# Hash attention and a gated feed-forward on one core: block loads of q and k as two transfers of 64 partitions, with three small edits

## The chip, the core and the metric

The kernel runs on one core of a Trainium2 chip. The metric is the device time of one execution in microseconds (us); lower is better.

## What is computed

Attention with a hash mask, then a feed-forward network on its result. Per batch (4) and head (8), with 768 tokens of 64 numbers:

```python
q_bits = (np.einsum('bhsd,dk->bhsk', q, proj) > 0)      # 6 bits a token
k_bits = (np.einsum('bhsd,dk->bhsk', k, proj) > 0)
mask = q_bucket[:, :, :, None] == k_bucket[:, :, None, :]
scores = np.where(mask, scale * np.matmul(q, k.transpose(0, 1, 3, 2)), -1e9)
attn = softmax(scores);  x = np.matmul(attn, v)          # then (3072, 512)
xn = x / sqrt(mean(x * x) + 1e-6) * rms_g
g = xn @ w_gate;  val = xn @ w_val                       # 512 -> 1536
out = (g * sigmoid(g) * val) @ w_out                     # 1536 -> 512
```

Inputs and output are 32-bit floats; the matmuls run in 16-bit floats.

## The kernel before

**Units and slots.** The 3072 tokens are eight units `w` of 384 rows: unit w is one half of batch w // 2. A unit has 8 heads, handled as four pairs `hp`. Three slots make one head of one unit, each with two score matmuls and one exponential over 768 keys' third: 192 slots in all. What else happens is hung on slots by hand: `at(s, f, ..., rank)` puts a step into slot s, and a final loop runs the slots in order, so the order of every engine's instructions is written out by this list. Each engine runs its instructions in that order.

**How q and k come in.** A pair (b, hp) of batch and head pair has three raw tiles, k, q and v. For batch 0 and the first two pairs of batch 1 they are loaded in rows (`load_rows`, line 117) and turned by TensorE. For the other ten pairs, from (1, 2) to (3, 3), q and k come by `load_blocks` (line 127): the 128 partitions of the tile are four blocks of 32, one for each of the two heads and each half of the 64 numbers d; a partition holds 24 tokens of 32 numbers, so a transfer is made of pieces of 128 bytes. VectorE then turns 32 x 32 blocks (`turn_dve`, line 205, four steps each for k and q), GpSimd casts the result into the score operands `QK` (line 213), and TensorE, VectorE and SP make the hash bits: products (line 221), signs (line 228) and sends of 12 rows into `QK` (lines 259, 279, 297 and 319). The slots of loads, turns, casts and hashes of these pairs stand in the table `work`.

**SP's queue.** SP issues all loads of q, k and v, the sends of bits, the transposes of x and the stores, in the order of the slots. Raw tiles come from a pool of nine buffers. GpSimd issues the weight loads.

**The feed-forward of a unit.** From slot s0 = 24 w + 42 on: gate (`g_ps`, line 479) and value (`v_ps`, line 489) products for twelve parts of 128 columns, then the output products (`y_ps`, line 502) for three chunks `c` of 128 rows each, and a store of each chunk (line 513). Before that, `scale_x` normalizes x (lines 447 and 452) and `turn_x` turns it, a chunk at a time: by a DMA transpose on SP's queue for the units of the list `BY_DMA` (line 458), or by four TensorE transposes (line 464) and one VectorE multiply (line 465) for the others. Before, unit 0 alone goes by TensorE.

Of the kernel before, what the change touches and what calls it, by code (L numbers as in the profile page):

```python
# [41 lines left out]
BY_PE = [(0, hp) for hp in range(4)] + [(1, 0), (1, 1)]  # L42


BY_DMA = (1, 2, 3, 4, 5, 6, 7)


@with_exitstack
def kernel(
# [48 lines left out]
    def bank(name, shape=None, dt=FP32):  # L98
        return gps.tile(shape or [128, 512], dt, name=name, tag="g")
# [4 lines left out]
    def raw_tile(b, hp, which):  # L104
        shape = [128, 24, 32] if which != "v" and (b, hp) not in BY_PE else [128, 2, 6, D]
        raw[b, hp, which] = lpool.tile(shape, FP32, name=which + "L", tag="L")
        return raw[b, hp, which]
# [13 lines left out]
    def load_blocks(eng, b, hp, which):  # L121
        lt = raw_tile(b, hp, which)
        for hh in range(2):
            src = {"q": q, "k": k}[which][b, 2 * hp + hh].rearrange("(t k) d -> t k d", k=24)
            for dc in range(2):
                p0 = 64 * hh + 32 * dc
                eng.dma_start(out=lt[p0 : p0 + 32], in_=src[:, :, 32 * dc : 32 * dc + 32])

# [38 lines left out]
    def out_chunk(w, c):  # L169
        b, half = divmod(w, 2)  # L170
        return 2 * c + half if b < 2 else 3 * half + c
# [271 lines left out]
    def scale_x(w, c):  # L443
        if w not in xn:
            xn[w] = npool.tile([128, 3, DMODEL], FP16, name="xn")
        if w in BY_DMA:
            nc.vector.scalar_tensor_tensor(  # L447
                out=xn[w][:, c, :], in0=x[w][:, c, :], scalar=rstds[w][:, c : c + 1],
                in1=grow, op0=ALU.mult, op1=ALU.mult,
            )  # L450
        else:
            nc.vector.tensor_scalar_mul(xn[w][:, c, :], x[w][:, c, :], rstds[w][:, c : c + 1])

    def turn_x(w, c):
        if w not in xnT:
            xnT[w] = npool.tile([128, 4, HALF], FP16, name="xnT", bufs=2)
        if w in BY_DMA:
            nc.sync.dma_start(  # L458
                out=xnT[w][:, :, c * 128 : (c + 1) * 128], in_=xn[w][:, c, :], transpose=True,
            )  # L460
            return
        ps = bank("x_ps", [128, 4, 128], FP16)
        for kt in range(4):
            nc.tensor.transpose(ps[:, kt, :], xn[w][:, c, kt * 128 : (kt + 1) * 128], ident16)
        nc.vector.tensor_mul(
            xnT[w][:, :, c * 128 : (c + 1) * 128], ps,
            gcol.unsqueeze(2).to_broadcast([128, 4, 128]),
        )
# [24 lines left out]
        )  # L493

    obank = {}

    def project(w, c, f0, f1):
        if f0 == 0:
            obank[w, c] = bank("y_ps")
        y = obank[w, c]  # L500
        for ft in range(f0, f1):
            nc.tensor.matmul(  # L502
                y, ht[w][:, ft, c * 128 : (c + 1) * 128], wo[:, ft, :],
                start=(ft == 0), stop=(ft == NF - 1),
            )
        if f1 == NF:
            b, half = divmod(w, 2)
            ysb = spool.tile([128, DMODEL], FP32, name="ysb", bufs=3)
            nc.scalar.copy(ysb, y)  # L509
            rows = out[b * S : (b + 1) * S, :].rearrange("(p c) n -> p c n", c=6)  # L510

            def store():
                nc.sync.dma_start(out=rows[:, out_chunk(w, c), :], in_=ysb)

            if (w, c) == (1, 0):
                at(86, store, rank=8)
            else:
                store()
            del obank[w, c]
# [100 lines left out]
    def at(s, f, *a, rank=3):  # L620
        plan[s].append((rank, len(plan[s]), lambda: f(*a)))
# [63 lines left out]
    def in_row(loads, s, hash_slot=None):  # L685
        return loads, range(s, s + 8), (s + 4, s + 8, s + 9), hash_slot

    work = {
        (1, 2): in_row((31, 32, 45), 49, 58), (1, 3): in_row((41, 43, 50), 56, 65),
        (2, 0): in_row((53, 55, 60), 64), (2, 1): in_row((66, 67, 68), 73, 82),  # L690
        (2, 2): in_row((72, 75, 78), 82), (2, 3): in_row((79, 86, 87), 90, 99),
        (3, 0): in_row((88, 91, 98), 100), (3, 1): in_row((94, 97, 112), 110, 119),
        (3, 2): in_row((115, 118, 124), 126), (3, 3): in_row((122, 125, 137), 136, 145),
# [1 line left out]
    for (b, hp), (loads, turns, cast_slots, sh) in work.items():  # L695
        for which, s in zip("kqv", loads):
            at(s, load_rows if which == "v" else load_blocks, nc.sync, b, hp, which)
        for i, s in enumerate(turns):
            at(s, turn_dve, b, hp, "kq"[i // 4], i % 4, rank=5)
        for which, s in zip("kq", cast_slots):  # L700
            at(s, cast_pool, b, hp, which)
        if sh:
            later = {(1, 2): (59, 7), (2, 1): (86, 7)}.get((b, hp), (sh, 3))
            if b == 1:
                at(sh, hash_lone, b, hp)
            else:
                at(sh, hash_pairs, b, (hp - 1, hp))
            at(later[0], lambda b=b, hp=hp: moves[b, hp](1), rank=later[1])
        late = 2 if (b, hp) == (2, 1) else 0
        at(cast_slots[2] + late, v_prep, b, hp)  # L710
        at(cast_slots[2] + late, v_sum, b, hp)
        if b > 1 and hp % 2:
            at(48 * b + (17 if hp == 3 else -8), v_mean, b, hp - 1, 4)
# [27 lines left out]
    for w in range(8):  # L741
        for h in range(H):
            end = LAST[w, h] + (2 if (w, h) == (0, 7) else 3)
            at(end - 1, av, w, h, 0, 9)
            at(end, av, w, h, 9, 18)
            if h % 2:
                if (w, h) == (1, 1):
                    at(end, o_first, w, 0, rank=4.5)
                    at(end + 3, o_last, w, 0, rank=4.5)
                else:  # L750
                    at(end, o_step, w, h // 2, rank=4.5)
                if (w, h) not in ((0, 5), (0, 7)):
                    late = 3 if h == 7 and w < 7 else 4
                    at(end + late, s_step, w, h // 2, rank=5)
        s0 = 24 * w + 42
        n0 = {0: 11, 2: 7, 3: 13, 4: 13, 5: 13, 6: 13}.get(w, 11)
        at(s0 - n0, norm, w, rank=5)
        for c in range(3):
            if w in BY_DMA:
                s = {1: (58, 58, 59), 2: (84, 84, 85), 7: (202, 202, 202)}.get(  # L760
                    w, (s0 - 11, s0 - 10, s0 - 9))[c]
                at(s, scale_x, w, c, rank=5)
                at(s, turn_x, w, c, rank=6)
            else:
                at(s0 - (6 if w == 0 else 8 - c), scale_x, w, c, rank=5)
                at(s0 - ((4, 3, 2) if w == 0 else (5, 3, 1))[c], turn_x, w, c, rank=1)
        seen = set()
        for ft in range(NF):
            for f, s in ((g_step, s0 + 16 * ft // NF), (v_step, s0 + (32 * ft + 16) // (2 * NF))):
                at(s, f, w, ft, rank=4 if s in seen else 2)  # L770
                seen.add(s)
        for i in range(9 if w < 7 else 6):
            c, j = divmod(i, 3)
            at(s0 + 16 + i, project, w, c, 4 * j, 4 * j + 4, rank=1 if i == 8 else 3)
# [55 lines left out]
```

## Time and profile before

| | |
|---|---|
| median of 3 runs | 329.36 us (328.5 to 330.08) |
| profiled execution | 327.8 us, its span 326.0 us |
| TensorE busy | 318.3 us, 98% of the span |
| VectorE, ScalarE, GpSimd busy | 70%, 64%, 51% |
| SP's transfer queue | 28.98 MB, 38.3% of 16 DMA engines' time |

Busy times are sums over the engine's instructions; "idle before, releaser" tells what ended an engine's wait. PE is TensorE, DVE VectorE, ACT ScalarE, POOL GpSimd, and SPq is SP's queue, which issues transfers. Lines of transfers count packets: under 512 B, under 2 KB and under 8 KB are counted cumulatively, and a queue's share is the time of its packets over 16 engines and the length of the window. Rows of a timeline begin with the start and the duration in us.

### The profile page before, as it was taken

To read this page: it belongs to the slowest core of one execution; us is meant where nothing else is said; L and a number is where in the kernel's file an instruction comes from. 1 tells how busy PE (TensorE), PEld (TensorE's weight loads), DVE (VectorE), ACT (ScalarE), POOL (GpSimd) and SP (SyncE) were. 2 spreads that over 40 slices of the span, in tenths; PEclk is the share of its full clock that TensorE was granted. 3 is DMA by queue.
4 is the path that set the end of the run, shared out by engine and by line. 5 is a ranking of instruction groups with operands and counts; after the bars stand their busy time and mean duration, and the time that the engine had idled before them with its cause. 6 is when DMAs were issued, how large, how long until landed. Compare 5 with 4: busy or idle time off the path is not lost.

```text
span 326.0 us, 7736 instructions
## 1 busy us (share of the span) xinstructions
PE 318.3 (98%) x2923; PEld 195.7 (60%) x2923; DVE 229.7 (70%) x513; ACT 208.1 (64%) x324; POOL 167.0 (51%) x238
## 2 busy tenths in 40 slices
PE   8998999999999999999999999999999999999995
PEld 7666766655565556655556656566566656654653
DVE  4798896889497985889387865967166834792860
ACT  3788986776575576657576766667577776422331
POOL 8887977279666786686844375733221320130000
PEclk9999999999999999999999999999999999999999
DMA  7998989985539825882470843002100021005002
GB/s 227 354 212 246 163 128 186 154 186 92 107 98 165 150 57 104 185 137 67 139 131 18 142 88 113 3 18 50 66 32 2 17 66 66 0 3 145 0 2 98
DMA packets 91813, 34.39 MB, mean 105 GB/s; under 512 B 76680, under 2 KB 88704, under 8 KB 91776
## 3 DMA queue, kind: packets, MB, share of 16 engines
q1 hardware_dynamic: 87696, 28.98, 38.3%
q0 software_dynamic: 3712, 4.72, 9.3%
q8 instruction: 23, 0.38, 0.5%
q10 hardware_dynamic: 368, 0.20, 0.2%
q14 instruction: 14, 0.11, 0.2%
HBM read 28.58 MB, written 6.29 MB: 107 GB/s over the span
## 4 chain that ended last, share of the span: by engine, by line
PE 88%; DMA 4%; SPq 3%; ACT 2%; DVE 1%; issue 1%; DVEq 0%; ACTq 0%
PE s_ps L363 18%; PE v_ps L489 18%; PE y_ps L502 17%; PE g_ps L479 14%; PE o_ps L385 10%; PE d_ps L221 4%; PE s_ps L479 4%; PE t_ps L181 2%; SPq L297 2%; DMA QK<-bits 2%; ACT psb L373 1%; PE z_ps L356 1%; DMA kL<-in_k_dram 1%; SPq L458 1%; DMA xnT<-xn 1%
## 5 line engine op out<-in xcount | busy, mean ns | idle before, releaser
L373 ACT ACTIVATE psb<-s_ps 128x768 f16<-128x768 f32 x192 | 150.7, 809 | 29.0 <-PE s_ps L363 27.2
L363 PE MATMUL s_ps<-QK 128*128 128x384 f16 (+1 forms) x384 | 93.6, 326 | 1.2 <-DMA QK<-bits 0.4
L489 PE MATMUL v_ps<-xnT,wv 128*128 128x384 f16 x384 | 78.1, 326 | 0.3 <-DVE t L490 0.2
L502 PE MATMUL y_ps<-wo,ht 128*128 128x512 f16 x276 | 68.7, 379 | 0.0
L412 POOL TENSOR_TENSOR x<-otmp,rcp 128x384 f32<-128x384 f32 x30 | 25.7, 858 | 83.2 <-DVE rcp L405 82.9
L490 DVE SCALAR_TENSOR_TENSOR t<-t,g_ps 128x384 f32<-128x384 f32 x78 | 42.9, 549 | 34.8 <-ACT t L481 34.7
L385 PEld LDWEIGHTS <-psb 128*128 128x128 f16 x1152 | 51.7, 97 | 22.5 <-issue 3.8
L481 ACT ACTIVATE t<-g_ps 128x384 f32<-128x384 f32 x78 | 38.2, 490 | 41.8 <-PE g_ps L479 37.2
L479 PE MATMUL g_ps<-xnT,wg 128*128 128x384 f16 x312 | 63.5, 326 | 0.0
L491 DVE SCALAR_TENSOR_TENSOR ht<-t,v_ps 128x384 f16<-128x384 f32 x96 | 53.2, 554 | 11.2 <-PE v_ps L489 1.1
L385 PE MATMUL o_ps<-vl,psb 128*128 128x65 f16 x1152 | 56.0, 193 | 0.4 <-DVE otmp L400 0.4
L489 PEld LDWEIGHTS <-wv 128*128 128x128 f16 x384 | 36.5, 98 | 23.5 <-issue 0.6
L479 PEld LDWEIGHTS <-wg 128*128 128x128 f16 x384 | 36.0, 98 | 23.7 <-DMA xnT<-xn 0.9
L502 PEld LDWEIGHTS <-ht 128*128 128x128 f16 x276 | 26.6, 98 | 27.9 <-issue 1.9
L363 PEld LDWEIGHTS <-QK 128*128 128x128 f16 (+1 forms) x384 | 31.1, 97 | 16.7 <-issue 3.1
L509 ACT COPY ysb<-y_ps 128x512 f32<-128x512 f32 x23 | 13.5, 585 | 22.1 <-PE y_ps L502 21.5
L400 DVE TENSOR_TENSOR otmp<-o_ps,cvb 128x390 f32<-128x390 f32 x32 | 17.9, 558 | 12.8 <-PE o_ps L385 12.8
L424 POOL TENSOR_TENSOR sq<-x 128x384 f32<-128x384 f32 x30 | 25.4, 847 | 2.4
L213 POOL CAST QK<-kT 64x768 f16<-64x768 f32 x20 | 17.0, 850 | 8.8 <-DVE kT L205 6.8
L213 POOL CAST QK<-qT 64x768 f16<-64x768 f32 x20 | 16.4, 820 | 9.5 <-DVE qT L205 8.8
L205 DVE STREAM_TRANSPOSE kT<-kL 128x192 f32<-128x192 f32 x40 | 19.6, 521 | 2.0 <-DMA kL<-in_k_dram 2.0
L447 DVE SCALAR_TENSOR_TENSOR xn<-x,rstd,grow 128x512 f16<-128x512 f32 x21 | 18.7, 906 | 0.9 <-POOL rstd L441 0.9
(81 smaller groups left out, 293.7 us busy)
## 6 DMA issues: line engine op xcount, KB each, us to landing
vL<-in_v_dram SPq DMA_DIRECT2D x16, 384.0 KB
out_dram<-ysb SPq DMA_DIRECT2D x23, 256.0 KB
kL<-in_k_dram SPq DMA_DIRECT2D x40, 96.0 KB
qL<-in_q_dram SPq DMA_DIRECT2D x40, 96.0 KB
kL<-in_k_dram SPq DMA_DIRECT2D x5, 384.0 KB
qL<-in_q_dram SPq DMA_DIRECT2D x5, 384.0 KB
wg<-in_moe_w_gate_dram POOLq DMA_DIRECT2D x2, 768.0 KB, 8.6
wv<-in_moe_w_val_dram POOLq DMA_DIRECT2D x2, 768.0 KB, 9.8
```

Source lines behind the costliest of these rows:

```text
L213: nc.gpsimd.tensor_copy(QK[b, hp][0:64, hh, o : o + S], T0[b, hp, which][64 * hh : 64 * hh + 64, :])
L363: nc.tensor.matmul(ps[:, j, 0:HALF], k_cols(w // 2, h, 2 * p + j), q_cols(w, h), start=True, stop=True,)
L373: nc.scalar.activation(psb[w, h][:, p], sps.pop(g)[:, :, 0:HALF], AF.Exp, scale=ESCALE,)
L385: nc.tensor.matmul(o[:, c, hh, 0:65], psb[w, h][:, jt // 2, jt % 2, 128 * c : 128 * c + 128], vls[b % 2][:, h, v_chunk(b, h, jt), 0:65], s ...
L412: eng.tensor_mul(xd.rearrange("p c (h d) -> p c h d", h=2), tmp[:, :, :, 0:64], r.to_broadcast([128, 3, 2, 64]),)
L424: nc.gpsimd.tensor_mul(sq, xd, xd)
L479: nc.tensor.matmul(g, wg[:, kt, fs], xnT[w][:, kt], start=(kt == 0), stop=(kt == 3))
L481: nc.scalar.activation(t, g, AF.Tanh, scale=0.5)
L489: nc.tensor.matmul(vv, wv[:, kt, fs], xnT[w][:, kt], start=(kt == 0), stop=(kt == 3))
L490: nc.vector.scalar_tensor_tensor(out=t, in0=t, scalar=1.0, in1=g, op0=ALU.add, op1=ALU.mult)
L491: nc.vector.scalar_tensor_tensor(out=ht[w][:, ft], in0=t, scalar=0.5, in1=vv, op0=ALU.mult, op1=ALU.mult)
L502: nc.tensor.matmul(y, ht[w][:, ft, c * 128 : (c + 1) * 128], wo[:, ft, :], start=(ft == 0), stop=(ft == NF - 1),)
```

## The change

Four edits. (1) `load_blocks` issues one transfer for each head of a pair, to 64 partitions, in place of two to 32; the source is ordered by half of d, then by token, so 40 transfers stand in place of 80, with the same pieces of 128 bytes. (2) The store of chunk 2 of unit 0 is hung on slot 69, behind the loads of pair (2, 1); so far it was issued as soon as it was made. (3) The turns of pair (2, 1) begin at slot 74 in place of 73, and its casts move with them. (4) Chunk 2 of unit 7 is turned by TensorE in place of a DMA transpose, and scaled without the row of weights, which its multiply applies.

```diff
-BY_DMA = (1, 2, 3, 4, 5, 6, 7)
+BY_DMA = [(w, c) for w in range(1, 8) for c in range(3) if (w, c) != (7, 2)]
...
-            src = {"q": q, "k": k}[which][b, 2 * hp + hh].rearrange("(t k) d -> t k d", k=24)
-            for dc in range(2):
-                p0 = 64 * hh + 32 * dc
-                eng.dma_start(out=lt[p0 : p0 + 32], in_=src[:, :, 32 * dc : 32 * dc + 32])
+            src = {"q": q, "k": k}[which][b, 2 * hp + hh]
+            eng.dma_start(
+                out=lt[64 * hh : 64 * hh + 64],
+                in_=src.rearrange("(t k) (c d) -> c t k d", k=24, c=2),
+            )
...
+    STORES = {(0, 2): 69, (1, 0): 86}
...
-            if (w, c) == (1, 0):
-                at(86, store, rank=8)
+            if (w, c) in STORES:
+                at(STORES[w, c], store, rank=8)
...
-        (2, 0): in_row((53, 55, 60), 64), (2, 1): in_row((66, 67, 68), 73, 82),
+        (2, 0): in_row((53, 55, 60), 64), (2, 1): in_row((66, 67, 68), 74, 82),
...
-            if w in BY_DMA:
+            if w:
...
                 at(s, scale_x, w, c, rank=5)
-                at(s, turn_x, w, c, rank=6)
+                if (w, c) in BY_DMA:
+                    at(s, turn_x, w, c, rank=6)
+                else:
+                    at(s0 - 4, turn_x, w, c, rank=1)
```

More of the change, by code (lines that the diff above doesn't have):

```diff
@@ L456, in turn_x @@
             xnT[w] = npool.tile([128, 4, HALF], FP16, name="xnT", bufs=2)
-        if w in BY_DMA:
+        if (w, c) in BY_DMA:
             nc.sync.dma_start(
@@ L758 @@
         for c in range(3):
-            if w in BY_DMA:
+            if w:
                 s = {1: (58, 58, 59), 2: (84, 84, 85), 7: (202, 202, 202)}.get(
@@ L762 @@
                 at(s, scale_x, w, c, rank=5)
-                at(s, turn_x, w, c, rank=6)
-            else:
-                at(s0 - (6 if w == 0 else 8 - c), scale_x, w, c, rank=5)
-                at(s0 - ((4, 3, 2) if w == 0 else (5, 3, 1))[c], turn_x, w, c, rank=1)
+                if (w, c) in BY_DMA:
+                    at(s, turn_x, w, c, rank=6)
+                else:
+                    at(s0 - 4, turn_x, w, c, rank=1)
+            else:
+                at(s0 - 6, scale_x, w, c, rank=5)
+                at(s0 - 4 + c, turn_x, w, c, rank=1)
         seen = set()
```

## The prediction

> **What bounds the kernel now.** I read the page's busy shares first, then the waits by stretch, then the transfers.
>
> ```profile
> span 326.0 us, 7736 instructions
> PE 318.3 (98%) x2923; PEld 195.7 (60%) x2923; DVE 229.7 (70%) x513; ACT 208.1 (64%) x324; POOL 167.0 (51%) x238
> q1 hardware_dynamic: 87696, 28.98, 38.3%
> 96.00:104.00 8.00, 7.36 (x66) 4.44 (x65) 5.67 (x13) 5.28 (x10) 5.33 (x8) 1.00 0.85 154
> 290.00:300.00 10.00, 9.56 (x48) 4.42 (x46) 3.65 (x7) 2.45 (x5) 0.73 (x1) 1.00 0.39 102
> ```
>
> TensorE is busy for 98% of the span, so as things stand only TensorE's own work and its 7.7 us of idle time set the end. The two windows below the page's lines (first number after the length: TensorE busy) hold the idle time that the change aims at: 0.64 us in one, 0.44 us in the other. The transfers of SP's queue (q1) take 38% of sixteen engines' time: hidden, but only while all sixteen share them. So three of the four edits can move tenths of a microsecond, and the fourth, the loads, can move far more if it changes how many engines share a load. That is what I price first.
>
> **The block loads: how many engines carry one.** Two windows of the trace, one with eight block loads and one store, one with eight sends of hash bits (12 rows each):
>
> ```profile
> DMA packets 6417, 1.07 MB, mean 112 GB/s; under 512 B 6288, under 2 KB 6288, under 8 KB 6416
> q1 hardware_dynamic: 6416, 1.05, 61.2%
> kL<-in_k_dram SPq DMA_DIRECT2D x4, 96.0 KB
> qL<-in_q_dram SPq DMA_DIRECT2D x4, 96.0 KB
> out_dram<-ysb SPq DMA_DIRECT2D x1, 256.0 KB
> ...
> DMA packets 192, 0.15 MB, mean 19 GB/s; under 512 B 96, under 2 KB 192, under 8 KB 192
> QK<-bits SPq DMA_DIRECT2D x8, 18.0 KB
> ```
>
> A block load of 32 partitions moves 32 x 24 pieces of 128 B: eight make 6144 small packets. The window has 6288; the other 144 are 16 for each of its nine transfers. In the second window eight sends move 96 rows, and there are 96 packets under 512 B beside them: 12 for each. So each transfer ends with one small packet from each engine that took part: 16 engines for a load of 32 rows, 12 for a send of 12 rows. The number follows the outermost count of the pattern; it is the largest number up to 16 that cuts it evenly.
>
> Now the diff. The old load had 32 partitions on one side and 768 pieces on the other, and 16 cuts both. The new one has 64 partitions at the destination, but its source is ordered "c t k d", and c, the outermost, counts 2 (the halves of d lie 128 B apart and can't be folded into t). If an engine has to take one even cut of both sides, two engines carry the whole load. If the destination alone decides, it is 16 as before. These are the ends. I take two: the engines that read and write are the same, and in the trace both sides of every transfer are cut in equal shares.
>
> The Trainium skill, page "DMA: Bandwidth & Descriptors", section "Why a DMA increments its semaphore by 16 and not by 1", says that of both patterns the slowest dimension that isn't 1 counts, and that the largest k up to 16 that divides both sizes is taken; its list of rules warns of an outermost dimension below 16 on either side. The 12 above agree with it; no run so far shows a transfer whose sides differ.
>
> **What a load then costs.** A store alone, by its window of 2.3 us, and the loads' window above, of 9.5 us:
>
> ```profile
> q1 hardware_dynamic: 144, 0.26, 30.4%
> out_dram<-ysb SPq DMA_DIRECT2D x1, 256.0 KB
> ...
> L127 SPq DMA_DIRECT2D kL<-in_k_dram x40: 566/655/2727, 31.4 to 181.4; - x40
> L127 SPq DMA_DIRECT2D qL<-in_q_dram x40: 566/644/2702, 39.4 to 184.8; - x40
> ```
>
> The store: 30.4% x 16 x 2.3 = 11.2 us of engine time, 0.70 us an engine. The loads' window: 61.2% x 16 x 9.5 = 93.0, less 11.2, is 81.8 us for 6272 packets: 13.0 ns each. An old load is 48 packets an engine, 0.63 us, and the queue issues one in 0.65 us (median of the rows). A new load is 1536 packets; on two engines 768 each, so 768 x 13.0 ns = 10.0 us. Ten pairs have four of them, 40 in all: 401 us on the same two engines, where the whole stretch from the first load to the last is now 31.4 to 184.8. No lead can hide that; the loads become the bound, and everything else that SP issues (hash bits, transposed x, stores) stands in line behind them. Issue times up to 2.7 us show that SP is held when the engines have enough to do, so the queue doesn't just run ahead.
>
> **The sum.** The chain after the change is: the first load, then SP's queue in its order to the last load, then the transposed x of unit 4, which stands right behind it, then TensorE from the first gate of unit 4 on.
>
> ```profile
> q0 software_dynamic: 2622, 3.14, 66.9%
> ...
> 75.09 3.16 SPq L297 DMA_DIRECT2D QK<-bits  x4
> 94.38 2.48 SPq L127 DMA_DIRECT2D kL<-in_k_dram  x3
> 113.17 3.24 SPq L319 DMA_DIRECT2D QK<-bits  x4
> 121.05 2.71 SPq L127 DMA_DIRECT2D qL<-in_q_dram  x4
> 123.86 4.11 SPq L319 DMA_DIRECT2D QK<-bits  x4
> 129.86 4.61 SPq L127 DMA_DIRECT2D kL<-in_k_dram  x4
> 145.18 6.78 SPq L319 DMA_DIRECT2D QK<-bits  x8
> 162.87 2.77 SPq L127 DMA_DIRECT2D kL<-in_k_dram  x4
> 172.36 6.41 SPq L319 DMA_DIRECT2D QK<-bits  x8
> 178.88 3.17 SPq L127 DMA_DIRECT2D kL<-in_k_dram  x4
> 186.21 5.30 SPq L458 DMA_TRANSPOSE xnT<-xn  x3
> ...
> 198.00 1.03 PE L502 MATMUL y_ps<-wo,ht 128*128 128x512 f16 x4
> 198.87 0.81 PE L479 MATMUL g_ps<-xnT,wg 128*128 128x384 f16 x4
> ```
>
> - Start of the first load: 31.4.
> - 40 loads: 401.
> - Other bytes on the same two engines: GpSimd's weight loads, 66.9% of the window 31.4 to 63, 21 us an engine; seven loads of v between the block loads at 1.05 (a store's 0.70 by size), grow and two stores: 10. Together 31.
> - Five stretches in which SP issues small transfers that wait for compute, while the two engines run empty: 75.1 to 94.4 (less 0.5 for the store that leaves it), 113.2 to 121.1, 123.9 to 129.9, 145.2 to 162.9, 172.4 to 178.9: 57 in all, if nothing is left in the queue; 0 if the queue always holds enough. I take 40, nearer to the upper end, since a load holds SP after a few transfers.
> - Transposes behind the last load: 5.3.
> - From the first gate of unit 4 to the end: 326.0 - 198.9 = 127.1. No block load is left there, and TensorE is as full as before.
>
> 31.4 + 401 + 31 + 40 + 5.3 + 127.1 = 636 us. The profiled execution took 327.8 us for its span of 326.0, so 1.8 lie around it: **638 us**. (The three runs' median is 329.4, 1.6 above that execution; this is inside the rounding of the terms.)
>
> **The other three edits.** The store of (0, 2) moves from before the loads of pair (2, 1) to behind them; the turns of that pair start a slot later; chunk 2 of unit 7 is turned by TensorE.
>
> ```profile
> 100.05 0.52 DVE L205 STREAM_TRANSPOSE kT<-kL 128x192 f32<-128x192 f32 x1 [1.95 <-DMA kL<-in_k_dram]
> 298.53 0.66 PE L479 MATMUL s_ps<-xnT,wg 128*128 128x384 f16 x3 [0.44 <-DMA xnT<-xn]
> L464 PE MATMUL x_ps<-ident,xn x12: 217/218/220, 44.6 to 46.2; 128*128 128x128 f16 x12
> ```
>
> The first two remove VectorE's wait of 1.95 us for kL, behind which the 0.64 us of TensorE's idle time lie: at best -0.6. The third removes the wait of 0.44 for the last transposed chunk and a transpose of SP's queue, and adds four matmuls of 0.218 on TensorE: +0.4. Its multiply on VectorE runs where VectorE is idle most of the time (3.65 of 10 us in the window shown), under the 7.9 us of TensorE's output matmuls; without that cover it would cost 0.7. With two-engine loads the first two are worth nothing, as the stall there is tens of microseconds, and +0.4 is lost in the rounding.
>
> **Rivals.**
>
> *Sixteen engines after all* (0.11). The destination's 64 partitions decide. A load is 96 packets an engine, 1.25 us, two in place of four: the same engine time, and 40 issues less on SP's queue, 26 us that TensorE doesn't wait for. Then only the small edits count: 327.8 - 0.6 + 0.4 = 327.6, not slower. It turns on one point: whether the source's 2 limits the cut. For it: no transfer of the trace has an outermost 2, so nothing shows that the source is asked. Against it: the even cuts above.
>
> *Two engines, but another two for each load* (0.05). A load lands 9.4 us later (10.0 - 0.63), but eight run beside each other and SP isn't held. The wait for kL at 100.05 grows by about 9; other pairs, with a few more us of lead, add 0 to 9 each: 337 to 351, say 345. For it: the trace doesn't say which engines a 12-row send uses. Against it: nothing in the trace shows a start that moves on from transfer to transfer; its chance is a guess. The same section of the Trainium skill says that the lowest-numbered k of the queue's engines are taken; no row here shows engine numbers.
>
> **How the numbers follow.** Two fixed engines: 0.84. Its range: the stretches at 0 and no price above 13.0 give 598; 4% less for the packet, whose price has only been seen with sixteen engines at work, 582; and if half of the weights' 21 us also hides, 572. The other way: the loads beside the weights, 31.4 to 47, cost more:
>
> ```profile
> q1 hardware_dynamic: 5164, 0.73, 30.7%
> ```
>
> 30.7% x 16 x 15.6 us / 5164 = 14.8 ns, which gives 40 x 768 x 14.8 = 455, 54 more, and the stretches at 57: 638 + 54 + 17 = 709. So 572 to 709, which leaves out the two rivals (0.16). About 0.5% (1.6 us) is what a measurement of this kernel tells from no change. Faster by more than that: 0.02, a part of the first rival. Within it: 0.09, the rest of that rival. Slower: 0.89.
>
> **What would show it.** Right: the page's DMA line shows one or two tenths for hundreds of microseconds (two of sixteen engines), with some 20 GB/s; each load leaves two small packets; issues of L125 take about 10 us each; TensorE's share falls to about half, and its waits are for hash bits and turns of blocks; from unit 4's first gate to the end stay 127 us. Wrong: issues of L125 of a microsecond and DMA shares as before (the first rival), or issues as short with landings some 10 us behind (the second). If the price is off, the time between landings of successive loads tells it: 10.0 us by my step.

## The result and the profile after

The changed kernel takes 555.7 us (552.3 to 556.8, six runs) against 328.5 for the one before: ratio 1.690, interval 1.684 to 1.697. The forecast was 638 with a range of 572 to 709: the mechanism came as forecast, the size didn't, and the result lies below the range.

The page of the kernel after: span, TensorE's share, its granted clock, transfers, and the chain that ended last.

```profile
span 554.2 us, 7689 instructions
PE 342.4 (62%) x2927; PEld 203.9 (37%) x2927; DVE 229.7 (41%) x514; ACT 208.4 (38%) x324; POOL 165.6 (30%) x238
...
PEclk9999658885569579756887556999655999999999
DMA  8986512122132131212312112311124011020101
...
DMA packets 90068, 34.24 MB, mean 62 GB/s; under 512 B 74936, under 2 KB 86960, under 8 KB 90032
q1 hardware_dynamic: 85952, 28.84, 21.9%
...
PE 43%; SPq 29%; DMA 17%; POOL 4%; DVE 2%; issue 2%; ACT 1%; DVEq 0%; POOLq 0%; ACTq 0%
```

TensorE falls from 98% of the span to 62%. For most of the span the sixteen DMA engines are busy to one or two tenths, and yet SP's queue and the transfers hold nearly half of the chain. What TensorE waited for, from the view of waits (us in total, times, longest):

```profile
PE s_ps L364 <- DMA QK<-bits: 89.7, 4, 37.3
PE g_ps L480 <- DMA xnT<-xn: 60.0, 2, 35.4
PE v_ps L490 <- DVE t L491: 29.6, 4, 10.5
```

The first two lines are transfers that came late, the third is VectorE, which stood waiting for blocks of k (70.3 us in six waits) before it came to TensorE's tile. Neither bits nor transposed x has become slower by itself: a send with nothing ahead of it still holds SP for 0.71 us, and the transfer of the transposed x that TensorE waits for takes 2.46 us, as against 2.45 before. They stand in SP's queue behind block loads. The loads' issues (min, median, max in ns), a stretch of SP's timeline, and the transfers of 10 us in which nothing but two-engine loads is under way:

```profile
L125 SPq DMA_DIRECT2D kL<-in_k_dram x20: 532/7144/19677, 31.5 to 389.9; - x20
...
298.76 15.05 SPq L125 DMA_DIRECT2D kL<-in_k_dram  x2
313.86 14.70 SPq L125 DMA_DIRECT2D qL<-in_q_dram  x2
328.66 7.09 SPq L117 DMA_DIRECT2D vL<-in_v_dram  x1
...
DMA packets 2088, 0.27 MB, mean 27 GB/s; under 512 B 2088, under 2 KB 2088, under 8 KB 2088
q1 hardware_dynamic: 2088, 0.27, 17.0%
```

A new load holds SP for 7.35 us (half of the 14.70); the two old ones whose place it takes held it for 0.65 each. Even the load of v behind them, spread over all engines, is held 7.1 us. The window from 180 to 190 us says why: 2088 pieces of 128 B in 10 us, 27 GB/s, the work of two engines. Each passes 104 pieces a microsecond, one in 9.6 ns.

### The profile page after: what moved, and what is told of

Its sections match the earlier page's. It is cut to its first block, busy times and chain, and to the rows that moved or that the text cites. A ratio compares the mean times of both kernels' runs of the same rounds, so it can differ in the third digit from the quotient of the medians.

```text
span 554.2 us, 7689 instructions
## 1 busy us (share of the span) xinstructions
PE 342.4 (62%) x2927; PEld 203.9 (37%) x2927; DVE 229.7 (41%) x514; ACT 208.4 (38%) x324; POOL 165.6 (30%) x238
## 4 chain that ended last, share of the span: by engine, by line
PE 43%; SPq 29%; DMA 17%; POOL 4%; DVE 2%; issue 2%; ACT 1%; DVEq 0%; POOLq 0%; ACTq 0%
SPq L125 15%; DMA kL<-in_k_dram 12%; PE v_ps L490 9%; PE s_ps L364 9%; PE y_ps L504 9%; PE g_ps L480 7%; PE o_ps L386 5%; SPq L117 4%; SPq L320 3%; SPq L298 2%; SPq L280 2%; PE s_ps L480 2%; SPq L459 2%; DMA QK<-bits 2%; PE d_ps L222 2%
## 5 line engine op out<-in xcount | busy, mean ns | idle before, releaser
L364 PE MATMUL s_ps<-QK 128*128 128x384 f16 (+1 forms) x384 | 98.7, 341 | 90.9 <-DMA QK<-bits 89.7
L480 PE MATMUL g_ps<-xnT,wg 128*128 128x384 f16 x312 | 68.3, 344 | 60.0 <-DMA xnT<-xn 60.0
L490 PE MATMUL v_ps<-xnT,wv 128*128 128x384 f16 x384 | 82.8, 341 | 29.6 <-DVE t L491 29.6
L504 PE MATMUL y_ps<-wo,ht 128*128 128x512 f16 x276 | 73.3, 397 | 9.2 <-DVE t L491 9.2
L480 PEld LDWEIGHTS <-wg 128*128 128x128 f16 x384 | 37.5, 101 | 86.5 <-issue 65.8
L386 PEld LDWEIGHTS <-psb 128*128 128x128 f16 x1152 | 54.7, 101 | 25.9 <-issue 9.8
L386 PE MATMUL o_ps<-vl,psb 128*128 128x65 f16 x1152 | 58.8, 197 | 0.9 <-DVE otmp L401 0.9
L490 PEld LDWEIGHTS <-wv 128*128 128x128 f16 x384 | 37.8, 101 | 55.8 <-issue 34.6
L206 DVE STREAM_TRANSPOSE kT<-kL 128x192 f32<-128x192 f32 x40 | 19.3, 514 | 70.3 <-DMA kL<-in_k_dram 70.3
L330 POOL CAST vl<-vL 128x768 f16<-128x768 f32 x16 | 13.2, 824 | 97.8 <-DMA vL<-in_v_dram 97.1
L206 DVE STREAM_TRANSPOSE qT<-qL 128x192 f32<-128x192 f32 x40 | 18.9, 511 | 42.4 <-DMA qL<-in_q_dram 42.4
```

Of the source, the lines that this page charges most:

```text
L206: nc.vector.transpose(dst.rearrange("p (c t r) -> p r c t", c=6, r=4)[:, r : r + 1], src.rearrange("p (r c) d -> p r c d", r=4)[:, r : r + 1],
L364: nc.tensor.matmul(ps[:, j, 0:HALF], k_cols(w // 2, h, 2 * p + j), q_cols(w, h), start=True, stop=True,)
L386: nc.tensor.matmul(o[:, c, hh, 0:65], psb[w, h][:, jt // 2, jt % 2, 128 * c : 128 * c + 128], vls[b % 2][:, h, v_chunk(b, h, jt), 0:65], s ...
L480: nc.tensor.matmul(g, wg[:, kt, fs], xnT[w][:, kt], start=(kt == 0), stop=(kt == 3))
L490: nc.tensor.matmul(vv, wv[:, kt, fs], xnT[w][:, kt], start=(kt == 0), stop=(kt == 3))
L504: nc.tensor.matmul(y, ht[w][:, ft, c * 128 : (c + 1) * 128], wo[:, ft, :], start=(ft == 0), stop=(ft == NF - 1),)
```

## The experiments

**The loads alone, and the small edits alone.**

```diff
# e2: the kernel before, with the new load_blocks
...
+                in_=src.rearrange("(t k) (c d) -> c t k d", k=24, c=2),
...
# e1: the changed kernel, with the old load_blocks
...
-                in_=src.rearrange("(t k) (c d) -> c t k d", k=24, c=2),
+            for dc in range(2):
+                p0 = 64 * hh + 32 * dc
+                eng.dma_start(out=lt[p0 : p0 + 32], in_=src[:, :, 32 * dc : 32 * dc + 32])
```

> The 40 new loads alone, without the three small edits. If the loads carry the whole loss: 555.7 us within 3, and each load leaves two small packets. If the small edits take part (the moved store, the later turns): 10 us or more away from that.

> The three small edits alone, with the old 80 block loads of 32 partitions. By every theory here the loss is in the loads, so this is the kernel before within 0.5%: 327.6 us against 327.8 (-0.6 for the wait for kL at 100 us, +0.4 for the four TensorE transposes of unit 7).

The loads alone: 556.8 us (one run). The small edits alone: 328.27 (12 runs), ratio 0.9956 to the kernel before, interval 0.9927 to 0.9984. So the loads are the whole loss. The edits took away both idle times that they aimed at; windows of e1, to be read beside those of the kernel before:

```profile
96.00:104.00 8.00, 8.00 (x80) 5.25 (x79) 6.52 (x14) 5.97 (x10) 6.56 (x9) 1.00 0.75 109
290.00:300.00 10.00, 10.00 (x54) 4.93 (x53) 4.66 (x10) 2.51 (x5) 1.05 (x2) 1.00 0.40 80
```

The loads alone also show the number of engines. Packets of the whole run, the kernel before and then e2:

```profile
DMA packets 91813, 34.39 MB, mean 105 GB/s; under 512 B 76680, under 2 KB 88704, under 8 KB 91776
...
DMA packets 90612, 34.38 MB, mean 62 GB/s; under 512 B 75480, under 2 KB 87504, under 8 KB 90576
```

1200 small packets less: 80 loads with 16 each were 1280, 40 with 2 each are 80.

**The same loads on 16, 2, 4 and 8 engines.** A load now takes one half of d for both heads: the heads lie behind each other in memory, so the source is one run of 1536 pieces. With the tokens in j interleaved sets its outermost count is j, with as many transfers, partitions and bytes. The numbers land in another order, so these kernels don't compute the reference's output.

```diff
...
-            src = {"q": q, "k": k}[which][b, 2 * hp + hh]
...
+        src = {"q": q, "k": k}[which][b, 2 * hp : 2 * hp + 2].rearrange("h s d -> (h s) d")
...
+                out=lt[64 * dc : 64 * dc + 64],
+                in_=src[:, 32 * dc : 32 * dc + 32].rearrange("(t k) d -> t k d", k=24),     # 16
+                in_=src[:, 32 * dc : 32 * dc + 32].rearrange("(t k j) d -> j t k d", k=24, j=J),  # 2, 4, 8
```

> As the changed kernel, with 40 loads of 64 partitions and 1536 pieces of 128 B, but each takes one half of d for both heads, so that its source has one outermost dimension of 1536 pieces (the numbers land in another order of partitions, so the output is not the reference's). Theory 1 (the source's outermost count sets the number of engines, and an engine passes a 128 B piece every 9.4 ns however many are at work, because its packets overlap): sixteen engines, 96 pieces each, landings of successive loads 0.90 us apart, time 327 to 328.5. Theory 2 (a piece takes 13 ns when sixteen engines crowd, 9.4 when two run): the same time, but landings 1.25 us apart. Theory 3 (the form of 64 partitions itself is slow, whatever the source's order): about 555 us.

> As the kernel with one half of d for both heads a load, but the tokens are taken in two interleaved sets, so that the source's outermost count is 2 again (numbers in another order, output not the reference's). Theories 1 and 2: two engines, landings 7.25 us apart, 555 us within 5. If it is the halves of d (addresses 128 B apart) that slow the loads, and not the count: 327 to 335.

> As the sixteen-engine kernel, but the tokens are taken in four interleaved sets, so that the source's outermost count is 4 (output not the reference's). If the count sets the engines: four, 384 pieces each, four small packets a load. If an engine passes a piece in 9.4 ns as long as few run: landings 3.6 us apart; in the changed kernel's chain 40 x 3.6 stands for 40 x 7.25, 145 us less: 411 us, 395 to 420. If a piece takes 13 ns from four engines on: 5.0 us apart, 466 us.

> The same with eight sets: source's outermost count 8, eight engines, 192 pieces each (output not the reference's). At 9.4 ns: landings 1.8 us apart, 72 us of loads, chain 218 us shorter than the changed kernel's: 338 us, 329 to 345. At 13 ns: 2.5 us apart, 366 us. Between the two tells at what number of engines the price of a piece begins to rise from 9.4 to the 13 of sixteen.

Times: 327.74 us with sixteen (ten runs; 0.9936 of before, interval 0.9911 to 0.9962), 560.7 with two, 413.2 with four, 349.0 with eight (one run each). The pages' packet counts, in the order 16, 2, 4, 8; all four have the same data:

```profile
DMA packets 90628, 34.25 MB, mean 105 GB/s; under 512 B 75496, under 2 KB 87520, under 8 KB 90592
...
DMA packets 90068, 34.24 MB, mean 61 GB/s; under 512 B 74936, under 2 KB 86960, under 8 KB 90032
...
DMA packets 90148, 34.24 MB, mean 83 GB/s; under 512 B 75016, under 2 KB 87040, under 8 KB 90112
...
DMA packets 90308, 34.24 MB, mean 99 GB/s; under 512 B 75176, under 2 KB 87200, under 8 KB 90272
```

Against two engines, four add 80 small packets, eight 240 and sixteen 560: over 40 loads that is 2, 6 and 14 more for each. For the counts tried, the source's outermost count sets the engines exactly; the 64 partitions are harmless, and halves of d (128 B apart) and tokens (256 B apart) cost the same within 1%.

How fast an engine then is, from SP's timelines of four, eight and sixteen engines (a row is two loads) and windows of pieces alone for four (206 to 218 us) and eight (158 to 165.5, then 188.5 to 193):

```profile
202.99 7.32 SPq L125 DMA_DIRECT2D kL<-in_k_dram  x2
210.35 7.42 SPq L125 DMA_DIRECT2D qL<-in_q_dram  x2
...
154.79 4.41 SPq L125 DMA_DIRECT2D kL<-in_k_dram  x2
159.25 4.47 SPq L125 DMA_DIRECT2D qL<-in_q_dram  x2
...
135.46 3.32 SPq L125 DMA_DIRECT2D kL<-in_k_dram  x2
138.82 2.97 SPq L125 DMA_DIRECT2D qL<-in_q_dram  x2
...
DMA packets 4937, 0.63 MB, mean 53 GB/s; under 512 B 4937, under 2 KB 4937, under 8 KB 4937
q1 hardware_dynamic: 4937, 0.63, 33.8%
...
DMA packets 5136, 0.65 MB, mean 87 GB/s; under 512 B 5136, under 2 KB 5136, under 8 KB 5136
q1 hardware_dynamic: 5136, 0.65, 72.8%
...
DMA packets 3484, 0.44 MB, mean 99 GB/s; under 512 B 3484, under 2 KB 3484, under 8 KB 3484
q1 hardware_dynamic: 3484, 0.44, 72.1%
```

Four engines: 12 us x 4 / 4937 = 9.7 ns a piece; eight: 7.5 x 8 / 5136 = 11.7 in the one window, 4.5 x 8 / 3484 = 10.3 in the other. In the stretches shown, loads follow each other after 7.35, 3.7, 2.2 and about 1.6 us with 2, 4, 8 and 16 engines. Two to four engines keep the same pace. With eight the time lies above the range expected (338, 329 to 345): at 10.3 to 11.7 ns in place of 9.4, 40 loads of 192 pieces an engine take 7 to 18 us longer, and 11 were missing. With sixteen neither theory fits as it stood: 96 pieces in 1.6 us is 16 ns, over the 13 of theory 2, but single slices of the window 136.8 to 141.4 us reach 216 GB/s, 9.5 ns on each of sixteen engines, and others fall to 10:

```profile
GB/s 197 196 193 181 185 169 113 97 71 44 25 16 10 71 149 209 216 198 339 196 196 148 60 10 100 149 116 160 198 199 214 205 151 129 47 17 19 19 22 27
```

So for a slice of 0.1 us at a time sixteen engines each keep the pace of two, but in this stretch they don't all have work all the time. Why not, wasn't separated. It costs this kernel nothing.

**Half of the loads.** New loads for k, the old four for q.

```diff
...
+        if which == "q":
+            ... # four transfers of 32 partitions, as before
+            return
```

> The changed kernel with the new loads for k alone; q is loaded by the old four transfers of 32 partitions. Half of the two-engine loads go: 20 x 7.25 = 145 us, and 40 old ones come back at 0.65, 26 us. If the cost is the sum of the loads one behind the other: 556 - 119 = 437 us, 425 to 445. If it lies in a few long stalls that one load would also make: over 500.

Measured: 435.3 us (one run). The cost is the sum of the loads, one behind the other.

**The same bytes in pieces of 256 B**, on two engines and on sixteen.

```diff
...
+                in_=src.rearrange("(t k j) d -> j t k d", k=12, j=2),       # two
...
+                in_=src[j].rearrange("(t k) d -> t k d", k=12),             # sixteen
```

> The changed kernel's 40 loads on two engines with the same bytes in pieces of 256 B in place of 128 (whole rows of d, tokens in two interleaved sets; output not the reference's): 384 pieces an engine. If an engine's price goes by the piece: landings 3.6 us apart, 411 us. If by bytes: 7.25 apart, 556 us. If as the packets' own recorded times (18 against 13 ns): 5.0 us apart, 466 us.

> Sixteen engines and the bytes of the 40 loads in pieces of 256 B (whole rows of d, even and odd tokens of both heads; output not the reference's): 48 pieces an engine and load. If sixteen engines are held back by pieces (15 ns each in the window of the 128 B kernel, 9.6 with two engines): landings 0.7 us apart, close to SP's issue time. If by bytes: 1.3 us apart as with 128 B. The time is 327 to 329 us either way.

Two engines: 499.6 us (one run), which is none of the three. The window 260 to 290 us of that kernel, then SP's timeline of the one with sixteen:

```profile
DMA packets 3878, 0.99 MB, mean 33 GB/s; under 512 B 3878, under 2 KB 3878, under 8 KB 3878
q1 hardware_dynamic: 3878, 0.99, 15.4%
...
132.37 2.01 SPq L127 DMA_DIRECT2D kL<-in_k_dram  x2
134.43 2.26 SPq L127 DMA_DIRECT2D qL<-in_q_dram  x2
```

30 x 2 / 3878 = 15.5 ns for 256 B against 9.6 for 128: 5.9 ns for the second 128 B and 3.7 that don't depend on the bytes, if those two points make a line. 384 x 15.5 ns is 5.9 us a load: 555.7 - 40 x (7.35 - 5.9) = 498. With sixteen, loads follow after 1.1 us, between the two expectations, and the time is 327.25 (one run), no different from the others with sixteen.

**The small edits one by one.**

```diff
# e8: the kernel before, with
+                at({(0, 2): 69, (1, 0): 86}[w, c], store, rank=8)
...
+        ... (2, 1): in_row((66, 67, 68), 74, 82),
# e7: the kernel before, with
+BY_DMA = [(w, c) for w in range(1, 8) for c in range(3) if (w, c) != (7, 2)]
...
```

> The kernel before with two of the small edits: the store of (0, 2) behind the loads of pair (2, 1), and that pair's turns a slot later. By my sum -0.6 us, 327.2 against 327.8 of the profiled execution, with TensorE's 0.64 us of idle time at 96 to 104 us gone. If the pair of edits carries the whole gain of the three edits (0.44%, interval 0.16 to 0.73%), 1.0 to 1.5 us.

> The kernel before with the third small edit alone: chunk 2 of unit 7 turned by TensorE. By my sum +0.4 us: 0.87 us of matmuls added, 0.44 of waiting for the last transposed chunk gone. If this edit carries the gain instead: 1.0 us or more faster than before.

Store and turns: 328.39 us, 0.9983 of before, interval 0.9961 to 1.0004. Unit 7: 328.67, 1.0019, interval 0.9986 to 1.0053. Each took away the idle time that it aimed at: in the profile of e8 TensorE is busy for all of the 8 us from 96, in that of e7 for all of the 10 us from 290. The ratios lie on the sides forecast (-0.6 and +0.4 us are 0.998 and 1.001), but neither interval excludes no change, and that of unit 7 hangs on three of its twelve runs (331.7 to 332.7); its median is below that of the kernel before. Which of them carries the 0.44% of e1 isn't settled either: e1's runs of the kernel before had a median of 330.0, these had 328.9.

## Why the prediction was right and where it was wrong

**Right: two engines, the same two for each load.** Two small packets a load, 27 GB/s, and loads that follow each other at 7.35 us refute both rivals as they were put: sixteen engines, and loads side by side with SP not held. That the two engines are the same for each load is inferred from this pace; no row shows engine numbers. What the Trainium skill's page "DMA: Bandwidth & Descriptors" says of k (section "Why a DMA increments its semaphore by 16 and not by 1") held for 2, 4, 8 and 16 on the source's side against 64 on the other. The second rival's own range had a fault: nine other pairs at 0 to 9 us each don't end at 351.

**Right: the chain.** First load, SP's queue to the last load, transposed x of unit 4, then TensorE alone. The first gate of unit 4 after the change:

```profile
425.20 1.44 PE L480 MATMUL g_ps<-xnT,wg 128*128 128x384 f16 x4 [35.36 <-DMA xnT<-xn]
```

Before that, the chain also runs through compute, in the stretches where SP's sends wait for it. This gate waited for the last transposed x, and from there to the end are 554.2 - 425.2 = 129.0 us, where the sum had 127.1. The four matmuls take 1.44 us where they took 0.81: the granted clock, 1.00 there in the kernel before, is 0.50 from 395 to 429 us.

**Wrong: the term "40 loads: 401".** The failing step is "768 x 13.0 ns = 10.0 us". I divided the queue's share of engine time by its packets and took the result as the time for which a packet keeps its engine. In the window of two engines 17.0% x 16 x 10 us are 27.2 us of packet time, and two engines have only 20 us: the records of an engine's packets overlap, 13.0 ns each at one every 9.6. 40 x 768 x 9.6 ns is 295 us, 106 less than the term. The same trace could have told: the kernel before has a window that sums to more than all of its engines' time (last two numbers: share and GB/s), and the slices of the very window that I priced from reach 215 GB/s on pieces of 128 B, 9.5 ns on each of sixteen engines:

```profile
8.00:40.00 32.00, 30.80 (x374) 21.52 (x374) 27.27 (x65) 27.43 (x41) 27.00 (x46) 1.00 1.03 245
...
GB/s 0 0 302 397 319 87 32 81 195 127 51 212 169 194 175 83 121 163 72 15 13 13 146 215 64 80 77 154 126 192 162 129 160 91 57 14 0 0 0 0
```

That SP issued an old load in 0.65 us, close to 48 x 13.0 ns, seemed to bear the price out. At 9.6 ns the same 48 pieces take 0.46 us, so that closeness was chance. The lower end of the range went wrong by the same step, since it let the price fall by 4% only.

**Too low: the rest.** From the first load to unit 4's first gate are 425.2 - 31.5 = 393.7 us; less 295 that leaves 99, where I had 31 for other bytes, 40 for the empty stretches and 5.3 for the transposes, 76. When the pieces of 128 B start, as the trace has it, shows where the 99 go. In my five stretches no piece of a block load starts for 17.7 us (154.7 to 172.4), 6.8 (249.8 to 256.6), 5.3 (271.6 to 276.9), 17.4 (336.7 to 354.1) and 7.0 (383.7 to 390.7): 54, close to the 57 that I had as the upper end, and not 40. A sixth stretch was missing, the sends of bits between the first pair's loads and the second's. The kernel before has it too (first three rows), and after the change (the other rows) no piece starts for 13.1 us there, 81.0 to 94.1:

```profile
46.86 6.17 SPq L279 DMA_DIRECT2D QK<-bits  x8
...
54.20 6.09 SPq L279 DMA_DIRECT2D QK<-bits  x8
60.40 3.15 SPq L127 DMA_DIRECT2D kL<-in_k_dram  x4
...
72.79 12.61 SPq L280 DMA_DIRECT2D QK<-bits  x8
85.50 0.46 SPq L117 DMA_DIRECT2D vL<-in_v_dram  x1
86.00 0.46 SPq L576 DMA_DIRECT2D grow<-in_moe_rms_g_dram  x1
86.56 6.08 SPq L280 DMA_DIRECT2D QK<-bits  x8
92.74 7.80 SPq L125 DMA_DIRECT2D kL<-in_k_dram  x2
```

Five shorter waits, of 0.5 to 2.4 us, add 7.5. So the empty stretches come to 74.7 where I had 40. What is left up to the last piece at 421.5, 20.3 us, is other bytes and slower pieces, where I had 31, and from there to the gate are 3.7, where I had 5.3.

With 9.6 ns and nothing else changed my sum would have been 532: under the result, where it had been over. The two errors ran against each other; with the rest right and the price at 13.0 ns the sum would have been 662. That 638 came no further from 555.7 was luck.

**The small edits.** With two-engine loads worth nothing, as forecast: e2 and the changed kernel differ by 1.1 us. Alone, the median of e1 is 1.8 us below that of its runs of the kernel before, where I had -0.2; the medians of the kernel before differ by 1.1 us between two sets of runs, so the size is uncertain. Of the versions that compute the reference e1 has the lowest median, 328.27, but e8's 328.39 can't be told from it.

## What to carry to other kernels

When two transfers are merged into one, look at the outermost count of both patterns: a short one that can't be folded away confined the whole transfer to as many engines here (2, 4 and 8), and one slow load in a queue delays everything issued behind it. A packet's recorded time is not the time that it takes from its engine: before a price is carried to other conditions, check whether the shares of a busy stretch sum to more than its engines have, and take the pace from packets per microsecond in a window that is really full.

## What the hardware showed that I had not expected

- An engine passes a piece of 128 B every 9.6 ns and one of 256 B every 15.5, with two engines at work; with eight, 10.3 to 11.7 for 128 B, and the records then grow to 15 to 17 ns each (72.1% x 16 x 4.5 us over 3484, 72.8% x 16 x 7.5 over 5136).
- TensorE's granted clock falls while it waits. It is 0.99 or 1.00 in every stretch of the kernel before. In the changed one it is 0.50 from 395 to 425 us, where TensorE does nothing, and 0.99 from 429 to 554, where it is busy for 121.7 us of 125. From 180 to 190 us it is 0.58 with 0.58 us of work (the number behind the counts is the clock):

```profile
180.00:190.00 10.00, 0.58 (x2) 0.25 (x2) 1.77 (x5) 0.00 (x0) 0.47 (x1) 0.58 0.17 27
```
